# Parts of k and q made in two pieces, a last store on one engine, and a loop count copied later

## The chip, the cores and the metric

One core of a Trainium2 chip runs the whole program. The metric is the device time of one execution in microseconds (us). Five engines run their own instruction queues in order: PE (matrix multiply; its weight loads are shown as PEld), DVE (vector), ACT (scalar, activations), POOL (GpSimd) and SP (issues most DMAs). They meet only at semaphores.

## The reference

Block-causal attention, and a two-level mixture of experts on its output, in float32:

```
scores = q @ k.T / 8                      # 8 batches, 8 heads, 576 rows, 64 columns
scores[block(i) < block(j)] = -1e9        # blocks of 64 rows
attn = exp(scores - max) / sum            # over a row
x = (attn @ v), heads side by side        # 4608 tokens x 512
g = argmax(x @ w_group); e = argmax(x @ w_expert[g])      # 4 groups of 4 experts
out[token] = p(g) * p(e) * (relu(x @ w1[g, e]) @ w2[g, e])
```

## The kernel before

The first 320 us are attention. A pair is two heads of one batch; there are 32 pairs, and one period handles one pair, with the neighbours' work mixed in by hand. The string `ORDER` lists tokens such as `S2@0` or `h0@-1a`: the letter names a step, the digit a part, the number behind @ how many periods the pair lies behind (-1 is the next pair), and a last `d` puts it on DVE instead of ACT or POOL. Each engine works its tokens off in this order. In the text, the period of pair x is the one in which S2 of pair x runs.

The steps that matter here:

- K transposes the first 512 rows of k and q of the next pair on PE; k0 and k1 evacuate them to `nf` on ACT (L284, L285). The last 64 rows are transposed at the end of V (L175) and evacuated by j0 and j1 on DVE (L281, L282).
- `high` (h0 for k, h1 for q; L194) rounds `nf` to the type that PE multiplies fast, on POOL. `low` (l0 for k on DVE, l1 for q on POOL; L199) is what the rounding left out. Each handles all 576 or 640 columns at once, so it also waits for j0 or j1.
- S computes scores as high times high, high times low, low times high (L228; S8, the last rows, is L218). D takes row maxima on DVE (L239), E the exponentials on ACT (L251), T transposes them on PE (L157), t evacuates on ACT (L284), V multiplies by v (L313), v evacuates the result to `xT` on DVE (L281).
- S2, T1, K, S3, V, T2, S1, T4, S8, T3 and the router's PE steps draw their outputs from one pool of four PSUM buffers in turn.
- Every fourth period begins a batch's routing: L, n, Y, M, then phases G0 to G4. G1 (`phase1`) multiplies `lgs` by `goh` (L751), then picks the expert (`pick`, L736 to L741: `edd`, `esc`, `eoh` have two inputs). G2 (`phase2`) makes `o16` (L763), then five running adds of 16 columns in bfloat16 (L769), then reciprocals (L780). G3 ends with L802 to L807. All of this is on DVE. R copies `ry` on POOL (L667). Z scatters a batch's table rows with an indirect DMA on POOL (L819). `caps` is ten small POOL steps in the period of pair 0.

From 320 us on, experts run in slots: h = relu(x w1) and y = h w2 on PE. A slot's rows are scaled by their routing weights (`store`, L1160 to L1165) and scattered to the output by an indirect DMA on POOL (L1167). The last slot's 128 rows are scaled half by ACT (L1160) and half by DVE (L1161).

Behind the slots stands a loop (`overflow`, L1341, L1342) over rows that did not fit; its count is one number, `cnti`, that `spill` copies on DVE (L646) long before the end. All engines load the count and skip or enter the loop, with semaphore instructions around it.

Of the kernel before, what the change touches and what calls it, by code (L numbers as in the profile page):

```python
# [8 lines left out]
F32 = mybir.dt.float32  # L9
# [4 lines left out]
AF = mybir.ActivationFunctionType  # L14
ALU = mybir.AluOpType
# [5 lines left out]
S = 576  # L21
BLK = 64
# [28 lines left out]

ORDER, ON_DVE = parse("""
Z2@7 E3@1 S2@0 D2@0 Z4@8 E2@1 n1@3a E8@1 T1@1 t3@1a t1@1a D0@0 K@-1 Z0@10 Y1@4 S3@0 D3@0 G2@6 R0@3
k0@-1a V@2 k1@-1a E0@0 E4@0 E5@0 E1@0 M1@4 E6@0 T2@1 S1@0 L0@3 E7@0 t2@1a T4@1 Z3@8 G1@5 S8@0 G0@4 j0@-1d G4@6
j1@-1d t0@1a Z1@9 h0@-1a v@2d L1@2 D1@0 l0@-1d D8@0 n0@3a G3@6 X0@4 X1@5 Y0@3 h1@-1a t4@1a M0@3 l1@-1a T3@0
X2@6
""")

# [9 lines left out]
class Attention:  # L68
# [119 lines left out]
    def side(self, tok):  # L188
        return self.nc.vector if tok in self.on_dve else self.nc.gpsimd

    def high(self, i, n, eng=None):
        r = self.rs[i]
        o = slice(S, 2 * S + BLK) if n else slice(0, S)
        (eng or self.side(("h", n))).tensor_copy(r["qk"][:, 0, o], r["nf"][:, o])  # L194

    def low(self, i, n, eng=None):
        r = self.rs[i]
        o = slice(S, 2 * S + BLK) if n else slice(0, S)
        (eng or self.side(("l", n))).tensor_tensor(out=r["qk"][:, 1, o], in0=r["nf"][:, o], in1=r["qk"][:, 0, o].bitcast(F32),  # L199
                                              op=ALU.subtract)  # L200

    PROD = ((0, 0), (0, 1), (1, 0))

# [120 lines left out]
    def start(self, N, order, on_dve, init):  # L324
        nc = self.nc
        self.load(0)
        self.wsb = self.pb[0][:, 0:256].bitcast(BF16)
        nc.vector.memset(self.wsb, 0.0)
        self.wps = self.wide("wps")[:, 0, :]
        self.warm(7)  # L330
        if N > 1:
            self.load(1)
        init()
        self.clear()
        self.on_dve = set()
        self.prep(0)
        self.on_dve = {("k", 1), ("j", 1)}
        self.values(-3, N)
        for n in range(2):
            self.full(0, n)  # L340
            self.full_last(0, n)
        self.on_dve = on_dve
        self.warm(5)
        self.high(0, 0, nc.vector)
        self.high(0, 1)
        self.low(0, 0, nc.vector)
        self.low(0, 1, nc.vector)
        if N > 2:
            self.load(2)

# [19 lines left out]
    def token(self, i, tok, N):  # L370
        k = tok[0]
        if not (-2 if k == "V" else k in "Kkjhl") <= i < N:
            return
        if k == "S":
            self.score(i, tok[1])
        elif k == "D":
            self.rowmax(i, tok[1])
        elif k in "tv":
            self.drain(i, tok)
        elif k == "E":  # L380
            self.expo(i, tok[1])
        elif k == "T":
            self.trans(i, tok[1])
        elif k == "V":
            self.values(i, N)
        elif k == "K":
            self.prep(i)
        elif k == "k":
            self.full(i, tok[1])
        elif k == "j":  # L390
            self.full_last(i, tok[1])
        elif k == "h":
            self.high(i, tok[1])
        elif k == "l":
            self.low(i, tok[1])
        elif i % 4 == 3:
            self.router.token(self, i // 4, tok)

# [7 lines left out]
R = 64  # L406
# [18 lines left out]
class Router:  # L425
# [96 lines left out]
    def ts(self, in0, s1, op0, s2=None, op1=None, sh=None, out=None, dt=F32):  # L522
        o = self.t(sh, dt) if out is None else out
        kw = {} if op1 is None else dict(op1=op1)
        self.nc.vector.tensor_scalar(out=o, in0=in0, scalar1=s1, scalar2=s2, op0=op0, **kw)
        return o

    def tt(self, a, b, op, sh=None, out=None):
        o = self.t(sh) if out is None else out
        self.nc.vector.tensor_tensor(out=o, in0=a, in1=b, op=op)  # L530
        return o

    def stt(self, a, s, b, op0, op1, sh=None, out=None):
        o = self.t(sh) if out is None else out
        self.nc.vector.scalar_tensor_tensor(out=o, in0=a, scalar=s, in1=b, op0=op0, op1=op1)
        return o
# [73 lines left out]
        self.res = res  # L610
        yield

    def spill(self, at, row, cnti):
        nc = self.nc
        V = nc.vector
        ts, tt, stt = self.ts, self.tt, self.stt
        one = [R, 1]
        x = tt(self.res[:, 1:2], self.cap, ALU.subtract, sh=one)
        xi = self.t(one, I32)
        ts(x, 0.0, ALU.max, P // UNIT - 1.0, ALU.add, out=xi)  # L620
        xi = ts(xi, (P // UNIT).bit_length() - 1, ALU.arith_shift_right, sh=one, dt=I32)
        ov = self.t(one)
        V.tensor_copy(ov, xi)
        st = stt(self.cap, float(UNIT), self.res[:, 2:3], ALU.mult, ALU.add, sh=one)
        rhs = self.t([R, 4, R])
        ts(self.trif, ov[:, 0:1], ALU.mult, out=rhs[:, 0:2, :])
        ts(self.c["ident"][0:R, 0:R], self.res[:, 0:1], ALU.mult, out=rhs[:, 2, :])
        ts(self.c["ident"][0:R, 0:R], st[:, 0:1], ALU.mult, out=rhs[:, 3, :])
        yield
        ps = at.psT("spill")  # L630
        nc.tensor.matmul(ps[0:R, 0:4 * R], lhsT=self.onesf, rhs=rhs.rearrange("p c r -> p (c r)"),
                         start=True, stop=True)
        yield
        g = self.t([R, 4, R])
        V.tensor_copy(g, ps[0:R, 0:4 * R].rearrange("p (c r) -> p c r", r=R))
        lo = ts(g[:, 1, :], self.pid[:, 0:1], ALU.is_le, sh=[R, R])
        ind = stt(g[:, 0, :], self.pid[:, 0:1], lo, ALU.is_gt, ALU.mult, sh=[R, R])
        stt(g[:, 1, :], -128.0, g[:, 3, :], ALU.mult, ALU.add, out=g[:, 3, :])
        ts(g[:, 3, :], self.p128[:, 0:1], ALU.add, out=g[:, 3, :])
        yield  # L640
        prod = tt(g[:, 2:4, :], ind.unsqueeze(1).broadcast_to([R, 2, R]), ALU.mult, sh=[R, 2, R])
        res = self.red(prod, sh=[R, 2])
        col = self.t([R, 2], I32)
        V.tensor_copy(col, res)
        nc.sync.dma_start(row, col)
        V.tensor_copy(cnti[0:1, 0:1], g[0:1, 0, R - 1:R])  # L646
        yield

    def token(self, at, b, tok):
# [193 lines left out]
class Moe:  # L843
# [302 lines left out]
    def store(self, s, c, full):  # L1146
        nc = self.nc
        ys = self.ro.rows.tile([P, 512], F32, tag="row", name=f"ys{s['n']}_{c}")
        n, y, cw = s["ch"][c][1], s["y"][c], s["ids"][:, c, 1:2].bitcast(F32)
        if not full:  # L1150
            tmp = self.ro.rows.tile([P, 512], F32, tag="row", name=f"yt{s['n']}")
            z = P - s["gap"]
            nc.scalar.activation(tmp[0:n], y[z:z + n], AF.Copy, scale=cw[z:z + n])
            while z:
                z -= s["gap"]
                src, tmp = tmp, tmp if z else ys
                nc.vector.scalar_tensor_tensor(out=tmp[0:n], in0=y[z:z + n], scalar=cw[z:z + n], in1=src[0:n],
                                               op0=ALU.mult, op1=ALU.add)
        elif s.get("o") == len(self.slots) - 1:
            nc.scalar.activation(ys[0:n, 0:256], y[0:n, 0:256], AF.Copy, scale=cw[0:n])  # L1160
            nc.vector.tensor_scalar(out=ys[0:n, 256:512], in0=y[0:n, 256:512], scalar1=cw[0:n], scalar2=None, op0=ALU.mult)  # L1161
        elif c % 2 == 0:
            nc.vector.tensor_scalar(out=ys[0:n], in0=y[0:n], scalar1=cw[0:n], scalar2=None, op0=ALU.mult)  # L1163
        else:
            nc.scalar.activation(ys[0:n], y[0:n], AF.Copy, scale=cw[0:n])  # L1165
        nc.gpsimd.memset(self.ro.mark, 0.0)
        i = nc.gpsimd.indirect_dma_start(  # L1167
            out=self.out, out_offset=bass.IndirectOffsetOnAxis(ap=s["ids"][0:n, c, 0:1], axis=0),
            in_=ys[0:n], in_offset=None, bounds_check=NTOK - 1, oob_is_err=False)
        self.ro.apart("out", i)  # L1170
# [191 lines left out]
def attention_moe(ctx, tc, q, k, v, w_group, w_expert, w1, w2, out, order=None, on_dve=None):  # L1362
    nc = tc.nc
# [11 lines left out]
    rowo = cp.tile([1, R, 2], I32, name="rowo")  # L1375
    cnti = cp.tile([1, 1], I32, name="cnti")
    inner = ExitStack()
    ET = mybir.EngineType
    with tc.manual_schedule(engines={ET.PE, ET.Activation, ET.DVE, ET.Pool, ET.SP}):
        ro = Router(tc, ctx, consts, w_group, w_expert, tab, xd)  # L1380
        moe = Moe(tc, ctx, consts, ro, w1, w2, out)
        at = Attention(tc, ctx, inner, q, k, v, consts)
# [49 lines left out]
            6: [lambda: b("X", 4), lambda: moe.getids(slots[1])],  # L1432
            7: [moe.grow_raw],
        }
        spl = ro.spill(at, rowo, cnti)
        for n in (60, 63, 65, 67, 68, 69):
            hooks[n] = [lambda: next(spl, None)]
        run = moe.run(hooks)
# [21 lines left out]
        b("G", 1)  # L1460
        for _ in run:
            pass
    moe.overflow(cnti, rowo)


# [24 lines left out]
```

## Time and profile before

| | us |
|---|---|
| median of 3 runs | 786.59 (786.25 to 786.68) |
| the profiled execution | 785.75 |
| its span, first to last instruction | 784.0 |
| PE busy | 759.1 |
| DVE busy | 544.7 |
| ACT busy | 500.4 |
| POOL busy | 350.2 |

Busy time says which engine has work, not which one the others wait for. A row of a timeline has start and duration in us, then engine, line, operation, output and inputs, shape and count; in square brackets stand the idle time of the engine just before it and what ended that. The granted clock of PE was 0.996 of full speed over the span.

### The profile page before, as it was taken

Reading aid. Unit: us, or ns where it says so; the run is one execution under the profiler, and the core shown is the slowest. Engines: PE = TensorE matmul, PEld = TensorE weight load, DVE = VectorE, ACT = ScalarE, POOL = GpSimd, SP = SyncE. Lnnn points to the kernel's source line nnn. Section 1 sums busy time; section 2 is a strip of 40 time slices with the busy share of each in tenths; the row PEclk is TensorE's granted clock in tenths of the full one; section 3 lists DMA queues with packets and bytes.
Section 4 is the critical chain, followed back from the end, with each engine's and each line's share of the span. In section 5 each row is a group of like instructions: output and inputs, shape, how many; then the busy total and the mean of one; then the engine's idle time right before and its main releaser. Section 6 shows DMA issues by size and latency. Waiting matters only on the chain.

```text
span 784.0 us, 20180 instructions
## 1 busy us (share of the span) xinstructions
PE 759.1 (97%) x7422; PEld 620.5 (79%) x7422; DVE 544.7 (69%) x1153; ACT 500.4 (64%) x1244; POOL 350.2 (45%) x481
## 2 busy tenths in 40 slices
PE   7899999999999999999999999999999999999996
PEld 4677777777777787768888788788988888888874
DVE  5567888888888888885454654754666667777742
ACT  5999999999999998755433433432434545545622
POOL 6444345454545454344143644454551553544212
PEclk9999999999999999999999999999999999999999
DMA  6478464646464636443779979979778897787771
GB/s 137 96 210 237 116 137 109 139 109 139 108 139 108 140 102 159 166 123 117 271 203 225 365 228 237 287 223 219 245 200 234 267 268 188 204 250 231 261 245 42
DMA packets 219108, 146.71 MB, mean 187 GB/s; under 512 B 155558, under 2 KB 186870, under 8 KB 219008
## 3 DMA queue, kind: packets, MB, share of 16 engines
q1 hardware_dynamic: 209920, 120.76, 57.6%
q0 software_dynamic: 9088, 24.64, 9.9%
q8 instruction: 60, 0.98, 0.5%
q14 instruction: 40, 0.33, 0.1%
HBM read 113.46 MB, written 24.59 MB: 176 GB/s over the span
## 4 chain that ended last, share of the span: by engine, by line
PE 80%; ACT 7%; DVE 6%; issue 3%; POOL 2%; DMA 2%; POOLq 0%; SPq 0%; ACTq 0%; DVEq 0%
PE h L1050 18%; PE y L1114 18%; PE o L313 10%; PE s L228 7%; PE tp L157 6%; PE h L1043 4%; PE s L218 3%; ACT pb L251 3%; PE ye L1114 3%; ACT pt L284 3%; PE he L1050 3%; PE y L1122 2%; DVE wl L949 1%; PE y L1133 1%; PE lg L690 1%
## 5 line engine op out<-in xcount | busy, mean ns | idle before, releaser
L1050 PE MATMUL h<-xt,wh 128*128 128x264 f32 (+6 forms) x704 | 156.3, 312 | 2.4 <-DVE xt L1010 2.3
L251 ACT ACTIVATE pb<-s,nm 128x128 f32<-128x128 f32 (+4 forms) x288 | 156.1, 568 | 3.5 <-DVE nm L239 1.6
L949 DVE TENSOR_TENSOR wl<-raw,wh 128x512 fp32r<-128x512 f32 x192 | 147.3, 804 | 8.5 <-ACT wh L948 8.4
L239 DVE TENSOR_REDUCE nm<-s 128x2 f32<-128x768 f32 (+4 forms) x160 | 126.3, 806 | 34.1 <-PE s L234 29.9
L1050 PEld LDWEIGHTS h<-xt,wh 128*128 128x128 f32 x704 | 119.2, 188 | 18.2 <-issue 4.2
L948 ACT CAST wh<-raw 128x512 fp32r<-128x512 f32 x192 | 109.6, 618 | 8.6 <-DMA raw<-in_moe_w_dram 6.0
L284 ACT COPY pt<-tp 128x1024 f32<-128x1024 f32 (+4 forms) x160 | 105.3, 696 | 8.6 <-PE tp L157 6.4
L1050 PE MATMUL h<-xt,wl 128*128 128x264 f32 (+6 forms) x352 | 109.2, 310 | 0.0
L1114 PE MATMUL y<-wh,hring 128*128 128x512 f32 x306 | 106.9, 400 | 0.4 <-ACT ys L1165 0.2
L228 PE MATMUL s<-qk 64*128 64x384 f32 (+3 forms) x768 | 89.9, 343 | 6.4 <-POOL qk L199 3.0
L1167 POOL DMA_INDIRECT out_dram<-ys,ids x40 | 47.0, 1174 | 108.1 <-DVE ys L1163 88.3
L313 PE MATMUL o<-pt,vb 128*64 128x320 f32 (+4 forms) x896 | 93.6, 360 | 0.4 <-DVE tmp L708 0.2
L194 POOL CAST qk<-nf 128x640 fp32r<-128x640 f32 (+1 forms) x63 | 42.7, 701 | 98.1 <-DVE nf L281 71.4
L313 PEld LDWEIGHTS o<-pt,vb 128*64 128x64 f32 x896 | 59.3, 137 | 32.2 <-DVE tmp L708 0.3
L157 PE MATMUL tp<-ident,pb 64*128 64x64 f32 x1600 | 76.3, 226 | 1.6 <-DVE xT L281 1.1
L228 PEld LDWEIGHTS s<-qk 64*128 64x128 f32 x768 | 61.6, 188 | 15.0 <-POOL qk L199 6.1
L157 PEld LDWEIGHTS tp<-ident,pb 64*128 64x128 f32 x1600 | 63.8, 140 | 10.2 <-ACT pb L251 3.9
L982 POOL COPY pl<-xg 128x1024 int16<-128x1024 int16 (+3 forms) x35 | 40.3, 1154 | 62.3 <-DMA xg<-xd,ids 40.6
L1114 PEld LDWEIGHTS y<-wh,hring 128*128 128x128 f32 x306 | 57.4, 188 | 13.1 <-DVE hring L1061 0.5
L1050 PEld LDWEIGHTS h<-xt,wl 128*128 128x128 f32 x352 | 66.2, 188 | 1.2
L251 ACT ACTIVATION_READ_ACCUMULATOR pb<-s,nm 128x1 f32 x288 | 64.1, 223 | 0.0
L199 POOL TENSOR_TENSOR qk<-nf,qk 128x640 fp32r<-128x640 f32 x31 | 61.2, 1975 | 2.6
(255 smaller groups left out, 1324.0 us busy)
## 6 DMA issues: line engine op xcount, KB each, us to landing
raw<-in_moe_w_dram SPq DMA_DIRECT2D x96, 512.0 KB, 4.2
rawq<-in_moe_w_dram SPq DMA_DIRECT2D x24, 512.0 KB, 7.8
natk<-in_k_dram SPq DMA_DIRECT2D x32, 256.0 KB, 3.6
natq<-in_q_dram SPq DMA_DIRECT2D x32, 256.0 KB, 5.5
vb<-in_v_dram SPq DMA_DIRECT2D x64, 128.0 KB, 2.8
wh<-in_moe_w_dram SPq DMA_DIRECT2D x16, 512.0 KB, 5.0
xd<-xns SPq DMA_DIRECT2D x12, 512.0 KB, 3.2
tab<-fill POOLq DMA_DIRECT2D x10, 512.0 KB, 4.1
```

The source lines that it names most:

```text
L157: self.nc.tensor.transpose(out=out[:, z], in_=src[r], identity=self.c["ident"][r, r])
L199: (eng or self.side(("l", n))).tensor_tensor(out=r["qk"][:, 1, o], in0=r["nf"][:, o], in1=r["qk"][:, 0, o].bitcast(F32), op=ALU.subtract)
L228: nc.tensor.matmul(st[:, z, :], lhsT=t[p, hq, S + P * u:S + P * u + P], rhs=t[p, hk, 0:w], start=x == 0 and c0 == 0, stop=False)
L239: self.nc.vector.tensor_reduce(out=o, in_=r["s", u], op=ALU.max, axis=ax, negate=True)
L251: nc.scalar.activation(reg, src, AF.Exp, bias=r["nm"][:, t:t + 1], accum_out=self.sms[b][:, pr, z, u:u + 1])
L284: return self.nc.scalar.copy(dst, src)
L313: nc.tensor.matmul(o[64 * a:64 * a + 64, hf, c0:c0 + BLK * (b1 - t)], lhsT=r["v"][:, a, j, :], rhs=pt[:, PTJ * j + t:PTJ * j + b1, a, :], ...
L948: nc.scalar.copy(h[:, sl], s["raw", u][:, sl])
L949: nc.vector.tensor_tensor(out=l[:, sl], in0=s["raw", u][:, sl], in1=h[:, sl].bitcast(F32), op=ALU.subtract)
L1050: nc.tensor.matmul(o, lhsT=ww[:, dc, f], rhs=rr[:, dc, t], start=dc == 0 and x == 0, stop=dc == 3 and x == 2)
L1114: nc.tensor.matmul(y[c][0:n], lhsT=hh, rhs=w, start=k == 0 and x == 0, stop=k == 7 and x == 2)
L1167: i = nc.gpsimd.indirect_dma_start(out=self.out, out_offset=bass.IndirectOffsetOnAxis(ap=s["ids"][0:n, c, 0:1], axis=0), in_=ys[0:n], in_o ...
```

## The change

- `high` and `low` work on named parts: `k` and `q` are the first 512 columns of each, `kt` and `qt` the last 64 and 128, `kq` both first parts in one instruction.
- h0 now makes the high parts of both first parts (one POOL copy of 2 x 512 columns) and stands right behind k1, followed by l1, the low part of q's first 512 columns, on POOL. l0 stays where it was, on DVE, with 512 columns. h1 (high parts of the last columns, where h0 stood) and the new l2 (their low parts, where h1 stood) are two small POOL instructions each.
- Pair 0, before the periods: high of k and both lows of the first parts on DVE, high of q and all last columns on POOL.
- The last slot's rows are scaled by ACT alone, 512 columns in one instruction.
- `spill` no longer copies the count; POOL copies it behind the last slot's scatter.

```diff
-k0@-1a V@2 k1@-1a E0@0 E4@0 E5@0 E1@0 M1@4 ... G1@5 S8@0 G0@4 j0@-1d G4@6
-j1@-1d t0@1a Z1@9 h0@-1a v@2d L1@2 D1@0 l0@-1d D8@0 n0@3a G3@6 X0@4 X1@5 Y0@3 h1@-1a t4@1a M0@3 l1@-1a T3@0
+k0@-1a V@2 k1@-1a h0@-1a l1@-1a E0@0 E4@0 E5@0 E1@0 M1@4 ... G1@5 S8@0 G0@4 j0@-1d G4@6
+j1@-1d t0@1a Z1@9 h1@-1a v@2d L1@2 D1@0 l0@-1d D8@0 n0@3a G3@6 X0@4 X1@5 Y0@3 l2@-1a t4@1a M0@3 T3@0

+    def part(self, t, n):
+        if n == "kq":
+            return t[:, 0:2 * S].rearrange("p (n c) -> p n c", c=S)[:, :, 0:512]
+        return t[:, dict(k=slice(0, 512), q=slice(S, S + 512), kt=slice(512, S), qt=slice(S + 512, 2 * S + BLK))[n]]
...
-        self.high(0, 0, nc.vector)
-        self.high(0, 1)
-        self.low(0, 0, nc.vector)
-        self.low(0, 1, nc.vector)
+        self.high(0, "k", nc.vector)
+        self.high(0, "q", nc.gpsimd)
+        self.low(0, "k", nc.vector)
+        self.low(0, "q", nc.vector)
+        for n in ("kt", "qt"):
+            self.high(0, n, nc.gpsimd)
+        for n in ("kt", "qt"):
+            self.low(0, n, nc.gpsimd)
...
         elif k == "h":
-            self.high(i, tok[1])
+            for n in ("kt", "qt") if tok[1] else ("kq",):
+                self.high(i, n, self.side(tok))
         elif k == "l":
-            self.low(i, tok[1])
+            for n in (("k",), ("q",), ("kt", "qt"))[tok[1]]:
+                self.low(i, n, self.side(tok))
...
-        V.tensor_copy(cnti[0:1, 0:1], g[0:1, 0, R - 1:R])
+        self.over = g[0:1, 0, R - 1:R]
...
-            nc.scalar.activation(ys[0:n, 0:256], y[0:n, 0:256], AF.Copy, scale=cw[0:n])
-            nc.vector.tensor_scalar(out=ys[0:n, 256:512], in0=y[0:n, 256:512], scalar1=cw[0:n], scalar2=None, op0=ALU.mult)
+            nc.scalar.activation(ys[0:n], y[0:n], AF.Copy, scale=cw[0:n])
...
         for _ in run:
             pass
+        nc.gpsimd.tensor_copy(cnti, ro.over)
     moe.overflow(cnti, rowo)
```

## Rows read from the trace of the kernel before

**Rows 1.** The page, busy time of each engine.

```profile
PE 759.1 (97%) x7422; PEld 620.5 (79%) x7422; DVE 544.7 (69%) x1153; ACT 500.4 (64%) x1244; POOL 350.2 (45%) x481
```

**Rows 2.** Waits: us in total, times, longest; PE (whole run), PEld (84 to 320 us).

```profile
PE s L228 <- POOL qk L199: 3.0, 4, 1.0
...
PEld s L228 <- POOL qk L199: 1.8, 8, 0.2
```

**Rows 3.** Waits of ACT, 16 to 64 us.

```profile
ACT pt L284 <- PE tp L157: 1.0, 2, 0.8
ACT pb L251 <- DVE nm L239: 0.7, 2, 0.5
```

**Rows 4.** Timeline, period of pair 16, ACT and DVE.

```profile
165.40 0.60 ACT L285 ACTIVATE nf<-tp 128x512 f32<-128x512 f32 x1
...
167.60 0.18 DVE L737 TENSOR_TENSOR edd<-el,emx 128x20 f32<-128x20 f32 x1
...
168.78 0.23 DVE L281 COPY nf<-o 128x64 f32<-128x64 f32 x1 [0.36 <-PE o L175]
...
169.12 0.75 DVE L281 COPY xT<-o 128x576 f32<-128x576 f32 x1
```

**Rows 5.** Timeline, period of pair 17, ACT, DVE, PEld and POOL.

```profile
174.67 0.60 ACT L285 ACTIVATE nf<-tp 128x512 f32<-128x512 f32 x1
...
176.12 0.23 DVE L763 TENSOR_TENSOR o<-goh,eoh 128x80 bf16<-128x80 f32 x1
...
176.50 0.97 DVE L769 TENSOR_TENSOR pre<-pre,o 128x16 bf16<-128x16 bf16 x5
...
178.25 0.19 DVE L281 COPY nf<-o 128x64 f32<-128x64 f32 x1
...
178.55 0.75 DVE L281 COPY xT<-o 128x576 f32<-128x576 f32 x1
...
181.55 0.52 DVE L805 TENSOR_TENSOR t<-t,o 128x80 f32<-128x80 f32 x1
...
179.41 0.83 PEld L218 LDWEIGHTS s<-qk 128*128 128x128 f32 x6 [0.20 <-PE tp L157]
...
178.57 1.33 POOL L194 CAST qk<-nf 128x576 fp32r<-128x576 f32 x2 [4.66 <-DVE nf L281]
179.98 1.99 POOL L199 TENSOR_TENSOR qk<-nf,qk 128x640 fp32r<-128x640 f32 x1
```

**Rows 6.** Timeline at 52 us; lines L805, L199: ns min/median/max, first and last start.

```profile
52.98 1.24 DVE L199 TENSOR_TENSOR qk<-nf,qk 128x576 fp32r<-128x576 f32 x1
...
52.87 0.73 POOL L194 CAST qk<-nf 128x640 fp32r<-128x640 f32 x1
...
L805 DVE TENSOR_TENSOR t<-t,o x8: 233/526/532, 103.1 to 352.3; 128x80 f32<-128x80 f32 x8
...
L199 POOL TENSOR_TENSOR qk<-nf,qk x29: 1537/1990/2118, 35.0 to 308.5; 128x640 fp32r<-128x640 f32 x29
L199 DVE TENSOR_TENSOR qk<-nf,qk x28: 736/748/1243, 43.7 to 308.4; 128x576 fp32r<-128x576 f32 x28
```

**Rows 7.** Timeline of the end; then lines L1165, L1341, L1342 and L1486 as above.

```profile
776.97 0.47 ACT L1160 ACTIVATE ys<-y,ids 128x256 f32<-128x256 f32 x1 [4.94 <-PE y L1114]
778.02 0.48 DVE L1161 TENSOR_SCALAR ys<-y,ids 128x256 f32<-128x256 f32 x1 [5.27 <-ACTq L1342]
778.79 0.99 POOL L1167 DMA_INDIRECT out_dram<-ys,ids  x1 [5.81 <-DVE ys L1161]
...
L1165 ACT ACTIVATE ys<-y,ids x11: 687/687/690, 434.0 to 767.8; 128x512 f32<-128x512 f32 x11
...
L1341 ACTq TENSOR_LOAD <-cnti x1: 465/465/465, 777.0 to 777.0; - x1
...
L1342 POOLq INC_SWDGE_SEM  x1: 943/943/943, 773.5 to 773.5; - x1
...
L1486 POOLq DRAIN  x3: 46/115/4631, 778.6 to 783.7; - x3
```

More of the change, by code (lines that the diff above doesn't have):

```diff
@@ L53 @@
 Z2@7 E3@1 S2@0 D2@0 Z4@8 E2@1 n1@3a E8@1 T1@1 t3@1a t1@1a D0@0 K@-1 Z0@10 Y1@4 S3@0 D3@0 G2@6 R0@3
-k0@-1a V@2 k1@-1a E0@0 E4@0 E5@0 E1@0 M1@4 E6@0 T2@1 S1@0 L0@3 E7@0 t2@1a T4@1 Z3@8 G1@5 S8@0 G0@4 j0@-1d G4@6
-j1@-1d t0@1a Z1@9 h0@-1a v@2d L1@2 D1@0 l0@-1d D8@0 n0@3a G3@6 X0@4 X1@5 Y0@3 h1@-1a t4@1a M0@3 l1@-1a T3@0
+k0@-1a V@2 k1@-1a h0@-1a l1@-1a E0@0 E4@0 E5@0 E1@0 M1@4 E6@0 T2@1 S1@0 L0@3 E7@0 t2@1a T4@1 Z3@8 G1@5 S8@0 G0@4 j0@-1d G4@6
+j1@-1d t0@1a Z1@9 h1@-1a v@2d L1@2 D1@0 l0@-1d D8@0 n0@3a G3@6 X0@4 X1@5 Y0@3 l2@-1a t4@1a M0@3 T3@0
 X2@6
@@ L189, in side, with high, low @@
         return self.nc.vector if tok in self.on_dve else self.nc.gpsimd
-    def high(self, i, n, eng=None):
+    def part(self, t, n):
+        if n == "kq":
+            return t[:, 0:2 * S].rearrange("p (n c) -> p n c", c=S)[:, :, 0:512]
+        return t[:, dict(k=slice(0, 512), q=slice(S, S + 512), kt=slice(512, S), qt=slice(S + 512, 2 * S + BLK))[n]]
+    def high(self, i, n, eng):
         r = self.rs[i]
-        o = slice(S, 2 * S + BLK) if n else slice(0, S)
-        (eng or self.side(("h", n))).tensor_copy(r["qk"][:, 0, o], r["nf"][:, o])
-    def low(self, i, n, eng=None):
+        eng.tensor_copy(self.part(r["qk"][:, 0], n), self.part(r["nf"], n))
+    def low(self, i, n, eng):
         r = self.rs[i]
-        o = slice(S, 2 * S + BLK) if n else slice(0, S)
-        (eng or self.side(("l", n))).tensor_tensor(out=r["qk"][:, 1, o], in0=r["nf"][:, o], in1=r["qk"][:, 0, o].bitcast(F32),
-                                              op=ALU.subtract)
+        eng.tensor_tensor(out=self.part(r["qk"][:, 1], n), in0=self.part(r["nf"], n),
+                          in1=self.part(r["qk"][:, 0], n).bitcast(F32), op=ALU.subtract)
     PROD = ((0, 0), (0, 1), (1, 0))
@@ L611, in final, with spill @@
         yield
-    def spill(self, at, row, cnti):
+    def spill(self, at, row):
         nc = self.nc
@@ L1434, in attention_moe @@
         }
-        spl = ro.spill(at, rowo, cnti)
+        spl = ro.spill(at, rowo)
         for n in (60, 63, 65, 67, 68, 69):
```

## The prediction

> **What bounds the kernel now.** I read the page's busy line first, then the waits of PE and ACT, then the timelines of two neighbouring periods, then the last microseconds. PE is busy 97% of the span [rows 1], so a gain has to show up as PE time. The first 320 us are 32 attention periods of some 9.3 to 10.2 us. In them PE waits for POOL's `low` of q (L199): four waits of 3.0 us on the matmul side in the whole run, and in the steady stretch 84 to 320 us eight of 0.2 us on the weight loads [rows 2]. These are what the change can remove. ACT has little room: from 16 to 64 us it waits 1.0 us for PE's transposes and 0.7 us for row maxima [rows 3]. A PE wait that ends when ACT still has its whole queue ahead of it buys nothing.
>
> DVE is the third engine that can set the end. In the period of pair 17, PE's weight load for S8 starts at 179.41, 0.11 us after DVE has evacuated `xT` (178.55 + 0.75 = 179.30), with 0.20 us of idle PE before it [rows 5]. The reason is in the code: four PSUM buffers go round, and V's output `o`, which `xT` empties, is the buffer that S8 takes after T2, S1 and T4. In the period of pair 16 `xT` ends at 169.87 [rows 4]. So what delays DVE ahead of `xT` delays PE.
>
> **The change, part by part.**
>
> *h0 and l1 on POOL, moved up behind k1.* Today POOL's `high` starts at 178.57 after 4.66 us of idle time, held by the evacuation of the last rows [rows 5]. After the change it needs only k1 (ACT, 174.67 + 0.60 = 175.27), so it starts there plus the 0.13 us that POOL takes today from a DVE evacuation's end to its start: 175.40. Its duration isn't shown: today's two copies, 1216 columns together, take 1.33 us [rows 5], so one of 1024 lies between half of that (0.67) and 1.33, and by columns it is 1.12. The subtract of 512 columns is 0.8 of the 640 that take 1.54 alone and 1.99 at the median [rows 6]: 1.2 to 1.6, I take 1.2. Both are done near 178 us, four microseconds before S2 at 182. **All waits of PE for L199 go.**
>
> What it gives: up to 64 us every idle ACT stretch in rows 3 lies behind a late S2 or behind a row maximum that queued after a DVE `low` slowed by POOL, so 1.7 us, bounds 0 and 3.0. In the steady stretch the 1.8 us are 0.3 for each of six rounds of four periods.
>
> *What POOL now runs beside.* DVE's router arithmetic used to run while POOL was idle. The trace shows what happens when a DVE operation with two SBUF inputs meets a POOL copy or subtract that has begun: it waits for the end of that instruction. DVE's `low` issued at 52.98 took 1.24 us (median 0.75), because POOL's `high` ran from 52.87 to 53.60 [rows 6]. L805, 80 elements, takes 0.23 us at least and 0.53 at the median; the one at 181.55 ends at 182.07, 0.10 us after POOL's subtract (179.98 + 1.99 = 181.97) [rows 5, 6].
>
> Pair 17 (phase 2, L763 on): today o16 at 176.12, five adds from 176.50, and `xT` at 178.55 without a break. After: POOL's copy runs 175.40 to 176.52, so o16 ends at about 176.62 instead of 176.35; the subtract has been waiting and goes next, 176.62 to 177.8; the first of the five adds, due to end at 176.69 (0.97 for five), ends 0.1 behind it, at 177.9. That is **1.2 us** on everything behind it on DVE: j0, j1, `xT` (179.30 to 180.5), D1. S8 follows `xT`, so PE loses the same, and ACT's next exponentials need D1.
>
> Pair 16 (phase 1): k1 ends at 165.40 + 0.60 = 166.00; copy 166.13 to 167.25, subtract to about 168.45. `edd` (two inputs, due at 167.60) ends near 168.5, 0.7 late; the 0.36 us of idle time ahead of `nf` takes half of it, and `xT` is **0.3 us** late [rows 4].
>
> The other two periods lose little: where R0's copies of `ry` stand ahead of h0 in POOL's queue, they hold it back until behind the router's work, and where phase 0 runs, its first two-input operation comes as the subtract ends. Z3's scatter now stands behind l1; nobody waits for it in that period.
>
> Phases 1 and 2 run in a period that still prepares a next pair for six batches (lag 5 and 6, pairs 3, 7, ..., 23). For each: 0.3 + 1.2 - 0.3 = 1.2; six give **+7.2 us**. Bounds: the new operands' wait isn't shown on bfloat16 adds of 16 elements, so below, only o16 and phase 1 wait (0.27 + 0.3 - 0.3, 1.6 us for six); above, nothing of the 0.3 comes back (9.0 us).
>
> The Trainium skill ("SBUF — State Buffer", section "SBUF: two separate sides") states that the port pair that DVE and GpSimd share is a lock held for the whole instruction, taken by whichever starts first, and names a DVE operation with two SBUF inputs against a GpSimd one that reads SBUF, with no exemption for size or type. The rows agree for the two operations that meet. By the page the bfloat16 adds wait too, and the term stays +7.2; by the rows alone the lower bound is open.
>
> *l0, l2, h1.* DVE's `low` has 512 columns instead of 576, about 0.08 us less, in a queue where S8 sets the next step: nothing. The four small POOL operations on 64 and 128 columns cost between 0.1 and 0.7 us each; they end long before S8 of the next pair, which alone needs the last rows. Nothing, unless they hold DVE's `low` (0.2 us).
>
> *The start.* Pair 0's `low` of q could end some 0.4 us sooner, but the small POOL operations now stand ahead of the ten steps of `caps` that precede pair 1's h0. I take 0, bounds -0.5 and +1.
>
> *The end.* Today ACT's half of the last `ys` ends at 777.44, DVE's half starts only at 778.02, behind DVE's own loop instructions, and the scatter at 778.79, 0.29 us after it; the span ends at 784.0 [rows 7]. After: ACT alone takes 0.69 for 512 columns, to 777.66; scatter at 777.95, 0.84 sooner, done issuing at 778.94. Then the copy of the count, its load (0.47), the branch and semaphore instructions that fill 777.44 to 778.02 today (0.58), and POOL's increment of 0.94 [rows 7] follow instead of running ahead: about 781.0. Behind that the 0.58 once or twice more, since all engines wait for each other there, and the 0.8 us from the end of POOL's long drain (778.6 + 4.6 = 783.2) to the span's end: 782.4 to 783.0. The handshakes from POOL's copy to five loads and back are in no row; for them I stay at 783.4. I take **-0.6**. If POOL's drain of 4.63 us is not just the wait for the scatter but has to be run behind the loop, it is +2.5 (781.0 + 4.6 + 0.8 = 786.4); the other end is -1.6.
>
> *The sum:* -1.7 + 7.2 - 0.6 = +4.9 us. The profiled execution took 785.75 us (span 784.0), and so would take 790.65; the median of the runs is 0.84 above it, 786.59, and the forecast on it is **791.5**.
>
> **The rivals.**
>
> *1. The waits go and nothing takes their place (faster).* Place: the same DVE queue, behind k1. If short DVE operations slip in between POOL's (small ones aren't held off for a whole copy), `xT` stays where it is. Then -1.7, six times up to 0.3 us (ACT idle behind the two late S2), -0.6: -4.1, 782.5. It decides at 0.3 us of late `xT` for each round; below that the round gets shorter. For it: no row shows a small bfloat16 add beside a POOL copy. Against it: L805 is small as well and waits.
>
> *2. Cancelled (within 0.2%).* The delay exists but half of it is taken back: L805's 0.3 us, which no longer meets a subtract, and 0.4 by a subtract that ends sooner or ACT catching up. 0.5 us is left for each round, 3.0 - 2.3 = +0.7, 787.3.
>
> *3. The change doesn't do what it says.* If S2's wait for q is on the whole tile, it goes to l2, late in the period: the stalls stay, the delay comes too, some 9 us, 796. Against it: PE waits for high and low apart today.
>
> **How the numbers follow.** A measurement here can tell 0.2%, 1.6 us, from no change. The case of the held-off router work has 0.53, its own range 788 to 795 (six times 0.7 to 1.5, end and early stretch within their bounds); rival 1 0.30 (781 to 785); rival 2 0.14; rival 3 0.03. The time is that of the first case. The range reaches down to rival 1's middle and up to where the first case ends: 782.3 to 794.8. Faster 0.31, within 0.14, slower 0.55.
>
> **What would show it.** Right: no wait of PE for L199 left; POOL's copy and subtract directly behind k1; the first L769 add or L763 of every round stretched from 0.2 us to about a microsecond, ending 0.1 us behind the subtract; S8's weight load in pair 17's period some 4.1 + 1.2 us behind k1; ACT idle ahead of its exponentials there; L805 at 0.23. In the end the last scatter 1.0 us behind the start of ACT's `ys`, and the loop's semaphores behind it. Wrong: `xT` at its old distance from k1 (179.30 - 175.27 = 4.03 us), or rounds of four shorter than today's.

## The result and the profile after

The changed kernel takes 793.85 us (median of 4 runs, 792.70 to 794.38) against 786.42 us (785.55 to 786.68) for the one before, measured side by side: a ratio of 1.0095, 95% interval 1.0080 to 1.0110. So it is slower, by some 7.4 us. The profiled execution took 794.38 us with a span of 792.5 us, 8.5 us longer than the span before.

Lines moved by about ten: `low` is L203, `high` L199, the row maxima L243, `xT` L285, `edd` L747, `o16` L773, the running adds L779, the last `ys` L1170, its scatter L1176, the copied count L1472, the loop L1351.

The page, first its busy line, answers to [rows 1].

```profile
PE 757.1 (96%) x7422; PEld 623.5 (79%) x7422; DVE 550.0 (69%) x1151; ACT 499.3 (63%) x1244; POOL 361.6 (46%) x579
```

PE's busy time fell by 2.0 us while the span grew by 8.5: PE waits more, and the busy line can't say for what. The waits of PE over the whole run, of ACT from 84 to 320 us, and of ACT in that stretch before, can (us in total, times, longest).

```profile
PE s L222 <- DVE xT L285: 7.6, 7, 1.3
...
PE s L232 <- POOL qk L199: 0.9, 1, 0.9
```

```profile
ACT pb L255 <- DVE nm L243: 7.2, 14, 0.9
ACT pt L288 <- PE tp L157: 3.8, 6, 1.1
```

```profile
ACT pb L251 <- DVE nm L239: 0.8, 2, 0.5
```

The four waits for the low parts of q [rows 2] are gone; one wait of 0.9 us for a high part is left in the first periods. In their place stands S8 (L222) waiting for `xT`, 7.6 us in seven waits. ACT's wait for row maxima in that stretch was 0.8 us in two waits before; now it is 7.2.

The ledger of the span, from the start of S2's first weight load in each period: S2 of pair 8 comes 1.0 us earlier (83.39 against 84.36); the six phase-2 periods (pairs 9, 13, ..., 29) take 66.3 us together instead of 60.1; the period of pair 26 takes 11.5 instead of 10.7; the rest up to the last matmul is 0.2 shorter; and from the last matmul to the span's end it is 9.8 us instead of 7.1. That is -1.0 + 6.2 + 0.8 - 0.2 + 2.7 = +8.5.

**A phase-2 period, pair 17.** Timelines of ACT, POOL, DVE and PEld in the changed kernel, in that order; they answer to [rows 5].

```profile
175.64 0.63 ACT L289 ACTIVATE nf<-tp 128x512 f32<-128x512 f32 x1
...
176.34 1.04 POOL L199 CAST qk<-nf 128x1024 fp32r<-128x1024 f32 x1 [3.02 <-ACT nf L289]
177.46 1.27 POOL L203 TENSOR_TENSOR qk<-nf,qk 128x512 fp32r<-128x512 f32 x1
...
177.04 0.43 DVE L773 TENSOR_TENSOR o<-goh,eoh 128x80 bf16<-128x80 f32 x1
...
177.61 1.95 DVE L779 TENSOR_TENSOR pre<-pre,o 128x16 bf16<-128x16 bf16 x5
...
180.64 0.75 DVE L285 COPY xT<-o 128x576 f32<-128x576 f32 x1
...
181.50 0.82 PEld L222 LDWEIGHTS s<-qk 128*128 128x128 f32 x6 [1.37 <-POOL qk L203]
...
182.08 0.47 ACT L255 ACTIVATE pb<-s,nm 128x256 f32<-128x256 f32 x1 [0.89 <-DVE nm L243]
```

POOL's copy now starts 0.07 us behind k1. `o16` was issued inside it and ends 0.1 us behind its end (0.43 us instead of 0.23). The five adds take 1.95 us instead of 0.97. Line by line one of the five carries all of that: 166 ns at least, 1150 at most, against 221 at most before. Lines of before, then of the changed kernel (ns min/median/max, first and last start):

```profile
L769 DVE TENSOR_TENSOR pre<-pre,o x40: 166/167/221, 98.1 to 349.7; 128x16 bf16<-128x16 bf16 x40
```

```profile
L779 DVE TENSOR_TENSOR pre<-pre,o x40: 166/166/1150, 97.2 to 355.6; 128x16 bf16<-128x16 bf16 x40
...
L815 DVE TENSOR_TENSOR t<-t,o x8: 229/230/231, 103.2 to 358.4; 128x80 f32<-128x80 f32 x8
```

That add starts at 177.61, in the middle of POOL's subtract, and ends at about 178.76, 0.03 us behind it. `xT` ends 5.12 us behind k1 (181.39 - 176.27) instead of 4.03, S8's weight load starts 0.11 us behind `xT` as before, with 1.37 us of idle time, and ACT's exponentials, which need the row maximum behind `xT`, have 0.89. The row names POOL's L203 as the releaser of S8; a small POOL subtract of the last rows happened to end just before. The matmul side names `xT`, and the constant 0.11 us bears that out. L815 has lost its collision, as foreseen [rows 6].

**A phase-1 period, pair 16.** POOL and DVE of the changed kernel, answering to [rows 4].

```profile
168.06 1.28 POOL L203 TENSOR_TENSOR qk<-nf,qk 128x512 fp32r<-128x512 f32 x1
...
168.59 0.79 DVE L747 TENSOR_TENSOR edd<-el,emx 128x20 f32<-128x20 f32 x1
...
170.26 0.74 DVE L285 COPY xT<-o 128x576 f32<-128x576 f32 x1
```

`edd` is held to 169.38, 0.04 us behind the subtract, and the period is 9.31 us, as before (9.33): what the hold-off costs, the missing gap in S2 gives back (no_subtract, below, has 9.16 without either).

**The period of pair 26**, which no step of the prediction named. It holds a few DVE steps for an early expert slot, one of them a subtract of two SBUF tiles of 16 columns (L540, L530 before). Lines of before, then POOL and DVE of the changed kernel:

```profile
L530 DVE TENSOR_TENSOR fin<-fin,eb x1: 153/153/153, 267.3 to 267.3; 64x16 f32<-64x16 f32 x1
```

```profile
271.25 1.05 POOL L199 CAST qk<-nf 128x1024 fp32r<-128x1024 f32 x1
...
271.39 0.94 DVE L540 TENSOR_TENSOR fin<-fin,eb 64x16 f32<-64x16 f32 x1
```

It was issued 0.14 us behind the start of POOL's copy and ends with it: 0.94 us instead of 0.15, and that period is 0.8 us longer.

**The end.** The timeline of ACT and POOL, then lines of POOL's queue (ns min/median/max, first and last start), of the changed kernel, answering to [rows 7].

```profile
782.77 0.69 ACT L1170 ACTIVATE ys<-y,ids 128x512 f32<-128x512 f32 x1 [4.94 <-PE y L1124]
...
783.74 0.98 POOL L1176 DMA_INDIRECT out_dram<-ys,ids  x1 [4.94 <-ACT ys L1170]
784.71 0.18 POOL L1472 CAST cnti<-fin 1x1 int32<-1x1 f32 x1
```

```profile
L1351 POOLq INC_SWDGE_SEM  x1: 975/975/975, 786.1 to 786.1; - x1
...
L1496 POOLq DRAIN  x3: 46/109/3257, 788.5 to 792.3; - x3
```

The scatter goes out 1.0 us behind the start of `ys`, as forecast. But POOL's drain begins only at 788.5, behind the loop's increment and its semaphores, and then still runs 3.26 us. Before, it began at 778.55, ahead of the scatter, and its 4.63 us covered that.

**The early stretch.** Windows of before, then of the changed kernel (PE, PEld, DVE, ACT, POOL busy; PE's granted clock; DMA share; GB/s).

```profile
18.00:23.10 5.10, 3.38 (x69) 2.60 (x65) 3.46 (x7) 5.10 (x17) 2.80 (x5) 1.00 0.68 136
23.10:26.50 3.40, 3.38 (x26) 3.11 (x28) 2.28 (x3) 3.19 (x10) 2.37 (x3) 0.50 0.40 72
```

```profile
18.00:22.20 4.20, 2.73 (x45) 1.96 (x45) 2.23 (x5) 4.20 (x16) 2.93 (x4) 1.00 0.81 141
22.20:29.00 6.80, 6.42 (x64) 6.08 (x66) 2.99 (x5) 5.52 (x15) 2.69 (x6) 0.50 0.26 49
```

PE ran at the lower of its two levels (1.2 of 2.4 GHz) for 3.4 us before and for 6.8 us after, each time behind a stretch at the full clock in which it had been busy 3.38 of 5.10 and 2.73 of 4.20 us. The period of pair 2 took 10.31 us instead of 9.27, and that ate part of the early gain in this execution. But the change does not set the length of that stretch: in a second trace of the same kernel (changed_again, below) it is 3.4 us, as before (24.3 to 27.8 us), and in end_only, with the attention of before, 6.8 us (11.4 to 18.2).

### The profile page after: what moved, and what is told of

It reads as the page before. It is cut to its first block, busy times and chain, and to the rows that moved or that the text cites. A ratio compares the mean times of both kernels' runs of the same rounds, so it can differ in the third digit from the quotient of the medians.

```text
span 792.5 us, 20254 instructions
## 1 busy us (share of the span) xinstructions
PE 757.1 (96%) x7422; PEld 623.5 (79%) x7422; DVE 550.0 (69%) x1151; ACT 499.3 (63%) x1244; POOL 361.6 (46%) x579
## 4 chain that ended last, share of the span: by engine, by line
PE 68%; ACT 11%; DVE 10%; issue 5%; POOL 3%; DMA 2%; SPq 0%; DVEq 0%; ACTq 0%
PE h L1060 18%; PE y L1124 18%; PE o L317 6%; ACT pt L288 5%; PE s L232 4%; ACT pb L255 4%; PE h L1053 4%; PE tp L157 3%; PE ye L1124 3%; PE he L1060 3%; PE s L222 2%; PE y L1132 2%; DVE nm L243 2%; DVE pre L779 1%; DVE wl L959 1%
## 5 line engine op out<-in xcount | busy, mean ns | idle before, releaser
L243 DVE TENSOR_REDUCE nm<-s 128x2 f32<-128x768 f32 (+4 forms) x160 | 126.2, 806 | 34.7 <-PE s L238 29.1
L199 POOL CAST qk<-nf 128x128 fp32r<-128x128 f32 (+3 forms) x96 | 51.9, 559 | 96.5 <-ACT nf L289 81.9
L1176 POOL DMA_INDIRECT out_dram<-ys,ids x40 | 47.2, 1179 | 104.5 <-DVE ys L1172 85.9
L232 PE MATMUL s<-qk 64*128 64x384 f32 (+3 forms) x768 | 87.8, 341 | 4.9 <-ACT pb L255 1.8
L232 PEld LDWEIGHTS s<-qk 64*128 64x128 f32 x768 | 63.2, 190 | 9.7 <-ACT pt L288 3.2
L255 ACT ACTIVATION_READ_ACCUMULATOR pb<-s,nm 128x1 f32 x288 | 66.0, 229 | 0.0
L203 POOL TENSOR_TENSOR qk<-nf,qk 128x64 fp32r<-128x64 f32 (+2 forms) x95 | 64.3, 690 | 2.6
```

The lines of the kernel that those rows point to most:

```text
L199: eng.tensor_copy(self.part(r["qk"][:, 0], n), self.part(r["nf"], n))
L203: eng.tensor_tensor(out=self.part(r["qk"][:, 1], n), in0=self.part(r["nf"], n), in1=self.part(r["qk"][:, 0], n).bitcast(F32), op=ALU.subtract)
L232: nc.tensor.matmul(st[:, z, :], lhsT=t[p, hq, S + P * u:S + P * u + P], rhs=t[p, hk, 0:w], start=x == 0 and c0 == 0, stop=False)
L243: self.nc.vector.tensor_reduce(out=o, in_=r["s", u], op=ALU.max, axis=ax, negate=True)
L255: nc.scalar.activation(reg, src, AF.Exp, bias=r["nm"][:, t:t + 1], accum_out=self.sms[b][:, pr, z, u:u + 1])
```

## The experiments

Two theories of the 8.5 us stood against rivals. For the attention: POOL's copy and subtract, moved beside the router's DVE work, hold off two-input operations on VectorE (the rival: it is the pieces, or something else in the new order). For the end: POOL has to drain behind its last work, wherever that stands (the rival: the drain belongs to the loop or to the scatter's transfer). Times differ a little between chips, and between two sets of runs on one (the kernel before has 788.30 and 786.90 us on the chip of the later experiments); each ratio is against the kernel before in the same set.

**attn_only** keeps the new `high` and `low` and takes the end back:

```diff
-            nc.scalar.activation(ys[0:n], y[0:n], AF.Copy, scale=cw[0:n])
+            nc.scalar.activation(ys[0:n, 0:256], y[0:n, 0:256], AF.Copy, scale=cw[0:n])
+            nc.vector.tensor_scalar(out=ys[0:n, 256:512], in0=y[0:n, 256:512], scalar1=cw[0:n], scalar2=None, op0=ALU.mult)
...
+        V.tensor_copy(cnti[0:1, 0:1], g[0:1, 0, R - 1:R])
```

> The change of k's and q's parts alone; the end is that of the kernel before (last slot's rows scaled by VectorE and ScalarE, the loop count copied early). Theory A (two causes that add: GpSimd's early copy and subtract hold off VectorE's adds, and the loop count copied late puts GpSimd's drain behind the loop): 5.8 us above before, all of it in the six phase-2 periods (+1.0 each) and in pair 26's period (+0.8), less 1.0 gained in the early stretch; last matmul to the end of the span 7.05 us again. Rival B (the end is no cause of its own, the loss is all in the attention stage and the later last matmul only shifts things): 8.5 us above before. Rival C (the end is all of it): no more than 1 us above before.

**end_only** is the other half: the kernel before with the new end.

```diff
+            nc.scalar.activation(ys[0:n], y[0:n], AF.Copy, scale=cw[0:n])
...
+        nc.gpsimd.tensor_copy(cnti, ro.over)
```

> The change of the end alone: the last slot's rows scaled by ScalarE alone, and the loop count copied by GpSimd behind the last scatter; k's and q's parts are those of the kernel before. Theory A: the drain of 4.6 us that GpSimd began 1.2 us before the scatter's issue ended now begins only behind the loop: 2.7 us above before, last matmul to the end of the span 9.7 us. Rival B (the prediction's first choice): 0.6 us below before. Rival C: the same as before within 0.5 us.

Measured: attn_only 791.27 us, +5.1 (ratio 1.0067, 1.0052 to 1.0081); end_only 788.75, +2.6 (1.0032, 1.0022 to 1.0041). The two add up to 7.7 us, the changed kernel's 7.4. Both halves cost, and theory A holds in both; attn_only lost 0.7 us less than expected, since its early gain was 1.9 instead of 1.0. In attn_only the phase-2 periods take 66.3 us again and the end 7.1; its S2 of pair 8 starts at 82.48, 1.9 us ahead of before, where the changed kernel with its longer slow stretch kept 1.0. In end_only the attention is that of before (60.1 us in phase 2) and the end is 9.8.

**rows_only** takes the new scaling by ACT alone; the count stays early.

```diff
+            nc.scalar.activation(ys[0:n], y[0:n], AF.Copy, scale=cw[0:n])
```

> Only the last slot's rows are scaled by ScalarE alone; the loop count stays early. Theory A: the scatter is issued with one wait fewer and the end comes 0.4 us earlier, or the time is the same within 0.5 us; the drain stays where it was. Rival: ScalarE's op over 512 columns is twice as long as over 256, so that the scatter is later and the end comes 0.2 to 0.4 us later.

Measured: 786.64 us, +0.5, which can't be told from nothing (1.0006, 0.9995 to 1.0017). From the last matmul to the end it is 7.0 us instead of 7.1. So all of the end's 2.6 us is the count that is copied late.

**no_loop** asks whether the drain belongs to the loop. It is rows_only without this line:

```diff
-    moe.overflow(cnti, rowo)
```

> The kernel before with the last slot's rows scaled by ScalarE alone and without the overflow loop: the loop for rows that don't fit in their slots, which these inputs run no time, is left out with the load of its count. Theory A (GpSimd's drain takes 3.3 to 3.4 us from the end of GpSimd's last work, the scatter's issue, whatever stands before it): the end is unchanged, the drain ends 3.4 us behind the scatter's issue, the time is 0 to 1 us below before. Rival B (the drain belongs to the loop and to its increment): the drain is shorter than 1 us, and the time is 2.5 to 3.5 us below before.

Measured: 787.43 us, ratio 0.9993 (0.9979 to 1.0008). From the last matmul to the end it is 6.5 us instead of the 7.0 of rows_only, because the scatter goes out 0.8 us sooner behind that matmul. The long drain of POOL's queue in end_only, then in no_loop:

```profile
L1486 POOLq DRAIN  x3: 46/109/3257, 783.2 to 787.0; - x3
```

```profile
780.26 0.99 POOL L1166 DMA_INDIRECT out_dram<-ys,ids  x1 [4.95 <-ACT ys L1160]
...
L1484 POOLq DRAIN  x3: 46/109/4621, 780.0 to 785.5; - x3
```

Without any loop the drain starts at 780.02 and ends at 784.64, 3.4 us behind the end of the scatter's issue (781.25). In end_only it starts at 783.18, 2 us after the scatter's data had landed (781.21), and takes 3.26 us all the same. Theory A: once POOL's work before it is done the drain takes 3.3 to 3.4 us, which are neither the loop's nor the transfer's wait; a loop that comes late is added ahead of it. What POOL does in that time no run shows.

**gated** keeps the pieces but puts POOL's copy of the first 512 rows back to the old place of h0, behind a piece that waits for j0, and the subtract of q to the old place of h1:

```diff
-k0@-1a V@2 k1@-1a h0@-1a l1@-1a E0@0 ... Z1@9 h1@-1a v@2d ... Y0@3 l2@-1a t4@1a M0@3 T3@0
+k0@-1a V@2 k1@-1a E0@0 ... Z1@9 h0@-1a v@2d ... Y0@3 l1@-1a t4@1a M0@3 h1@-1a l2@-1a T3@0
...
-            for n in ("kt", "qt") if tok[1] else ("kq",):
+            for n in ("qt",) if tok[1] else ("kt", "kq"):
```

> The pieces of the change (first 512 rows of k and q apart from their last rows) with the copy at the old place of h0, behind a piece that waits for j0, and the subtract of q at the old place of h1; the end is that of the kernel before. Theory A (it is the place of GpSimd's copy and subtract beside VectorE's first adds that costs, not that they are made in pieces): the phase-2 periods are 10.0 us again, the first add of a router round takes 0.2 us, and the time is 0 to 3 us below before. Rival B (the pieces themselves cost: more GpSimd instructions, and each one's start): 2 to 6 us above before, with the phase-2 periods over 10.5 us wherever GpSimd stands.

Measured: 787.12 us (1.0010, 0.9995 to 1.0024): the loss is gone, the forecast gain did not come. Five of the phase-2 periods are 9.8 to 9.9 us and phase 1 is 9.15, both 0.2 shorter than before, and no add takes over 222 ns. But four of the phase-0 periods (pairs 11, 15, 19, 23) take 10.0 instead of 9.72, those of pairs 7 and 9 lose 0.95 and 0.8, and those of pairs 4 and 6, in the early stretch, 0.8 and 0.6. POOL and DVE in gated, in the period of pair 10, which delays the next one, and in that of pair 17:

```profile
112.46 1.28 POOL L203 TENSOR_TENSOR qk<-nf,qk 128x512 fp32r<-128x512 f32 x1
...
112.58 1.71 DVE L203 TENSOR_TENSOR qk<-nf,qk 128x512 fp32r<-128x512 f32 x1
...
180.66 1.83 POOL L203 TENSOR_TENSOR qk<-nf,qk 128x512 fp32r<-128x512 f32 x1
...
180.67 0.68 DVE L203 TENSOR_TENSOR qk<-nf,qk 128x512 fp32r<-128x512 f32 x1
```

In the first two rows DVE's own `low` is the victim: issued 0.12 us behind POOL's, it takes 1.71 us instead of 0.68. In the last two they start 0.01 us apart, DVE keeps its 0.68, and it is POOL's that takes 1.83. It is so ahead of pair 27 too, and that phase-0 period takes 9.72 us.

**gated_qt** puts one small copy between, so that DVE's `low` should start first:

```diff
-... Y0@3 l1@-1a t4@1a M0@3 h1@-1a l2@-1a T3@0
+... Y0@3 h1@-1a l1@-1a t4@1a M0@3 l2@-1a T3@0
```

> The gated version with the copy of q's last 128 columns put between GpSimd's copy of k and q and its subtract. Theory A (the same holding off cuts both ways: in the gated version's phase-0 periods VectorE's own subtract of k, 0.68 us alone, was issued 0.12 us behind GpSimd's subtract and took 1.71): VectorE's subtract now begins 0.15 us before GpSimd's, is 0.7 us in every period, the six periods of pairs 11, 15, 19, 23, 27, 7 are 9.7 us instead of 10.0 (and the two of pairs 7 and 9 some 0.8 shorter), and the time is 2 to 3.5 us below the gated version, 0.3% below before. Rival B (the periods of 10.0 us come from elsewhere, from GpSimd being late for the next pair): no change against the gated version, or up to 2 us more where GpSimd's subtract is now 0.3 us later.

Measured: 787.66 us against 788.30 on that chip (0.9993, 0.9980 to 1.0005). The two single losses are gone (9.73 and 9.77 us), but phase 0 is 10.27 us where no_loop, whose attention is that of before, has 9.87 in the same set of runs. The rows that go with it, POOL and DVE in the period of pair 10:

```profile
109.32 2.42 POOL L203 TENSOR_TENSOR qk<-nf,qk 128x512 fp32r<-128x512 f32 x3
...
109.33 1.83 DVE L203 TENSOR_TENSOR qk<-nf,qk 128x512 fp32r<-128x512 f32 x1
```

Here, and in the periods of pairs 14, 18, 22 and 30, the two still start at most 0.01 us apart, and this time DVE's is held: where the lead was needed, mostly ahead of phase 0, the edit did not bring it about. In the other nineteen periods from pair 7 on it did: DVE's starts 0.10 to 0.12 us ahead and keeps its 0.68, and POOL's takes 1.71 instead of 1.28. One of them is that of pair 26, and the phase-0 period behind it, that of pair 27, takes 10.27 us all the same. So the holding off is not all that lengthens phase 0 here; what the rest is stays open. No version beat the kernel before by what can be measured.

**no_subtract, one_fill, writes_only and subtract_twice** vary the one suspect, POOL's subtract behind k1: left out, replaced by one or by three fills of its output, or done twice.

```diff
-            for n in (("k",), ("q",), ("kt", "qt"))[tok[1]]:
+            for n in (("k",), ("q", "q"), ("kt", "qt"))[tok[1]]:
```

> The changed kernel with GpSimd's subtract of q done twice in a row, the same values both times. Theory A (VectorE's adds are held off for as long as GpSimd's instruction lasts, and GpSimd's next one goes ahead of VectorE's next): a second add of each phase-2 round is stretched to 1.1 to 1.3 us, the six phase-2 periods grow from 11.05 to 12.2 us, those of phase 1 by 0.3 to 1.2, so 7 to 14 us above the changed kernel. Rival B (GpSimd's work at that place costs only the one collision that the first subtract makes, and VectorE passes once it has its turn): 0 to 2 us above the changed kernel.

That was subtract_twice; the next is writes_only. one_fill has the fill once, no_subtract only in the first two periods.

```diff
+            if tok[1] == 1:
+                t = self.part(self.rs[i]["qk"][:, 1], "q").bitcast(F32)
+                for _ in range(3):
+                    self.nc.gpsimd.memset(t, 0.0)
-            for n in (("k",), ("q",), ("kt", "qt"))[tok[1]]:
+            for n in (("k",), (), ("kt", "qt"))[tok[1]]:
```

> The changed kernel with GpSimd's subtract of q replaced by three fills of its output with zeros: the low part of q's first 512 rows is left out. GpSimd is about as busy, at the same place, but reads nothing from SBUF. Theory A (any GpSimd instruction that has begun holds off VectorE's two-input adds): the first add of pair 17's round is stretched to the length of a fill, 0.3 us or more, in total as far as 0.5 to 1.2 us, and the phase-2 periods stay between 10.5 and 11.1 us. Theory B (only a GpSimd instruction that reads SBUF does): the first add takes 0.2 us beside the fills, xT ends 4.0 to 4.3 us behind k1, the phase-2 periods are 10.0 to 10.2 us and the time is 5 to 6 us below the changed kernel.

> The changed kernel without GpSimd's subtract of q behind k1 (the low part of q's first 512 rows is left out, filled with zeros once for each of two buffers); the copy stays at its place. Theory A (GpSimd's SBUF reads beside VectorE's two-input operations are what costs; the copy alone holds off only o16, by 0.2 to 0.3 us): the phase-2 periods are 10.0 to 10.2 us, phases 0 and 1 stay at 9.7 and 9.3, pair 26's period 10.7 to 11.0, and the time is 5 to 7 us below the changed kernel, its end of 9.75 us unchanged. Rival B (something else in the new order lengthens the periods): phase 2 stays over 10.6 us, or phases 0 and 1 grow to 10.2 and more as in the version with three fills.

> The changed kernel with GpSimd's subtract of q replaced by one fill of its output with zeros (the low part of q's first 512 rows is left out); one of about 0.55 us instead of three. In the version with three fills the phase-2 periods were 10.0 us but those of phases 0 and 1 were 10.7 and 10.2 instead of 9.7 and 9.3, with PE's transposes of T2 signalled about 1.0 us behind their last row while GpSimd issued a scatter. If the length of GpSimd's fills, or where they put its scatter, makes that: phases 0 and 1 come back to 9.7 and 9.3. If it is that GpSimd's subtract is gone at all: they stay at 10.2 and more.

**changed_again** is the changed kernel on the chip of no_subtract and one_fill.

> The changed kernel once more, for its trace on the same chip as the two versions without the subtract: periods of 9.7, 9.3, 11.0 and 10.2 us, 1.15 us for the first add, as in its first trace. If a chip has other periods in phases 0 and 1, it shows here.

Periods in us, from S2 to S2 (phase 0 of pair 19, phase 1 of pair 20, phase 2 of pair 21), and the time:

```
                 phase 0  phase 1  phase 2   time     before on that chip
changed             9.73     9.33    11.08   793.85   786.42
changed_again       9.72     9.32    11.08   794.55   786.90
no_subtract         9.73     9.16    10.00   786.62   786.90
one_fill            9.73     9.15    10.00   786.07   786.90
writes_only        10.68    10.19    10.04   797.54   788.30
subtract_twice     10.82    10.85    12.64   820.72   788.30
```

Without the subtract the phase-2 period is 10.00 us, and the kernel is back at the time before (ratio 1.0005, 0.9985 to 1.0024), although it still has the late end's 2.7 us. This settles the cause of the six periods: the gain against the changed kernel is a little over the 5 to 7 us expected (7.9 against changed_again, 7.2 by the medians). POOL's fills and the running adds in writes_only, the lines of all its adds, and the same stretch of a phase-2 period in subtract_twice:

```profile
177.14 1.69 POOL L407 MEMSET qk<- 128x512 f32 x3
...
177.43 0.97 DVE L783 TENSOR_TENSOR pre<-pre,o 128x16 bf16<-128x16 bf16 x5
...
129.04 0.80 ACT L288 COPY pt<-tp 128x768 f32<-128x768 f32 x1 [1.13 <-PE tp L157]
```

```profile
L783 DVE TENSOR_TENSOR pre<-pre,o x40: 166/167/221, 95.2 to 357.4; 128x16 bf16<-128x16 bf16 x40
```

```profile
186.04 0.43 DVE L773 TENSOR_TENSOR o<-goh,eoh 128x80 bf16<-128x80 f32 x1
...
186.61 2.93 DVE L779 TENSOR_TENSOR pre<-pre,o 128x16 bf16<-128x16 bf16 x5
...
186.46 2.65 POOL L203 TENSOR_TENSOR qk<-nf,qk 128x512 fp32r<-128x512 f32 x2
```

Beside three fills in a row (1.69 us of POOL's time, at the same place) the five adds take 0.97 us, and no add is held: 221 ns at most. A POOL instruction that only writes does not do it, one that reads does, and each further one holds one more add: 0.97, 1.95, 2.93 us for the five adds with no, one and two subtracts. The Trainium skill says this in "SBUF — State Buffer", section "SBUF: two separate sides": a VectorE operation with two SBUF inputs meets the exclusive lock only against a GpSimd operation that reads SBUF. The trace agrees, also for bfloat16 adds of 16 columns (1150 ns beside the subtract, 167 beside the fills), which the rows before left open.

Two sizes were missed. subtract_twice lost some 25 us more than the changed kernel's 7.4 where 7 to 14 were expected, since phases 0 and 1 lost 1.1 to 1.5 us each as well: in phase 1 `eoh` was held besides `edd` (0.94 us instead of 0.18), in phase 0 `goh` (0.93 instead of 0.18). Some 0.15 and 0.25 of it no_loop shows in the same set with the attention of before. And writes_only was slow for another reason: phases 0 and 1 took 0.6 to 0.8 us more than in no_loop in the same set (9.87 and 9.56), with ACT waiting 1.13 us for PE's transposes T2 (the last row of its timeline above) while POOL issued a scatter. With one fill instead of three this is gone, but one_fill belongs to the later set, in which changed_again has its usual periods. In no_loop, with no fill at all, PE reports late too: in phase 0 DVE's copy of the last rows starts 0.23 to 0.26 us behind PE's last of them, just after a scatter, instead of the 0.04 of before. So the fills alone are not the cause, and why PE reports late stays open. In one_fill PE's clock was 1.00 through the early stretch, and S2 of pair 8 came at 81.75, another 1.7 us sooner than in no_subtract (83.43); no experiment set the clock apart.

## Why the prediction was right, and where its sizes were off

The forecast was 791.5 us, slower by 4.9; it came out at 793.85, slower by 7.4. The mechanism is the one that it put first, and its term by term account reads:

- *All waits of PE for L199 go.* Right in S2 but for one of 0.9 us in the first periods. The copy started 0.07 us behind k1 instead of 0.13 and took 1.04 instead of 1.12; the subtract 1.27 instead of 1.2.
- *Phase 2, 1.2 us on everything behind the first add.* `xT` is 1.09 us later, the period 1.03 longer, six times: +6.2. Rival 1, that short DVE operations slip in between, fails on the 1150 ns of one add; in no_subtract, where nothing holds the adds, the period is back at 10.00 us.
- *Phase 1, 0.3 late, and 0.3 given back for a round.* Both halves were about 0.16: no_subtract has 9.15 to 9.16, before and after 9.31 to 9.33. The net of nothing was right. With phase 2, the term of +7.2 measured +6.2, 1.0 too much.
- *Pair 26.* +0.8, missing from the sum. The prediction looked for two-input DVE operations in the router's phases only; `early` has one as well, and the copy alone holds it (the period stays 11.5 to 11.6 without the subtract). This miss nearly makes up for the 1.0 above, so that the attention's total came out close (+5.1 in attn_only against -1.7 + 7.2 = +5.5) is in part luck.
- *The early stretch, -1.7.* The sign was right, the size is not settled: attn_only shows -1.9, the changed kernel -1.0 and again -1.1. S2 of pair 8 starts at 84.25 to 84.60 us in the four traces whose attention is that of before, and at 81.63 to 83.43 in the seven with the copy behind k1. In the first trace of the changed kernel PE's longer stay at 1.2 GHz goes with the difference: S2 of pair 2 starts at 25.1 us there as in attn_only, and the period takes 10.31 instead of 9.34. In changed_again that stay was no longer than in attn_only, and S2 of pair 1 came 0.8 us later (16.73 against 15.91), why stays open. The working is not borne out either: ACT's waits of 1.7 us, of which all were to go, are 0.7 in attn_only and 2.0 in the changed kernel.
- *The end, -0.6.* This is the step that failed, on the wrong side: +2.7. The prediction named the bound, "if POOL's drain of 4.63 us is not just the wait for the scatter but has to be run behind the loop, it is +2.5", and chose the other reading. [Rows 7] alone could not decide it, since there the drain runs beside the scatter; end_only did. (The terms of the bound add up to +2.4.) That the bound comes so close is in part luck: it charged all 4.63 us of the drain, 1.2 of which lay beside the scatter, and left out the 1.4 us that pass in the changed kernel between the end of the loop's increment (787.06) and the drain's start (788.46).
- *The start, 0.* S2 of pair 1 came 0.5 us sooner, one end of its bounds; it is part of the -1.0. In changed_again it came 0.7 us later, and in end_only, with the attention of before, 0.9 later, so a single trace does not size this term.
- Rival 2 (half taken back) and rival 3 (S2's wait goes to l2) fail with the six periods and with the vanished waits.

With the end at +2.7 and pair 26 at +0.8 the sum would have been +9.0 by its own terms, against 8.5 in the profiled execution.

## What to carry to other kernels

An engine's idle time can be what keeps another engine fast: before moving GpSimd work into it, list every VectorE operation with two SBUF inputs in that stretch, in every kind of period, rare ones included, and charge each with the rest of the GpSimd instruction that it meets, if that one reads SBUF. At the end of a program, ask which engine's drain ends last, and keep what that engine still waits for off the path. Here that was a loop whose count came late; no run copied the count late on another engine, and since all engines load it, it is open whether that would have cost less. When one change joins two edits, run each alone: here both lost, for unrelated reasons, and the wanted early gain of 1 to 2 us stood behind them.

## What was not expected of the hardware

- POOL's final drain takes 3.26 us although nothing is outstanding any more (end_only: the scatter had landed at 781.21, the drain ran from 783.18 to 786.43), and 3.4 us from the end of a scatter's issue when it starts before it.
- The hold-off works both ways, and which engine pays is decided by less than the trace resolves: of two subtracts that start 0.01 us apart, DVE's took 1.83 us instead of 0.68 in gated_qt, POOL's 1.83 instead of 1.28 in gated. With 0.10 to 0.12 us between them the first kept its time on either engine: DVE's behind POOL's took 1.71 in gated, POOL's behind DVE's 1.71 in gated_qt.
- PE's granted clock of 0.50 lasted 3.4, 6.8 and 0 us in three versions of nearly the same early work (before, changed, one_fill), and 6.8 and 3.4 us in two executions of the changed kernel itself.
